# SwiGLU on one core: ScalarE's load of the first gate slices in two parts, behind its first Silu

## The chip, the core and the metric

The kernel runs on one core of a Trainium2 chip. The core has five engines with instruction queues of their own: TensorE (PE in the profile; its weight loads are listed apart as PEld), VectorE (DVE), ScalarE (ACT), GpSimd (POOL) and SyncE (SP). SP, ACT and POOL also issue DMAs from their queues. The metric is device time in microseconds, lower is better.

## The reference

```python
B, S, D, F = 1, 2048, 640, 1536      # all bf16
def reference(x, w_gate, w_up, w_down):
    g = _silu(x @ w_gate)            # [S, D] @ [D, F]
    u = x @ w_up
    return (g * u) @ w_down          # [S, F] @ [F, D]
```

## The kernel before

The rows of x are worked in four blocks of 512 (`S_BLK`, NSB = 4). D = 640 is cut into KD = 5 pieces of 128 (the contraction index `kd`, 0 to 4), F = 1536 into KF = 12 slices of 128 (the index `fc`). All weights stay in SBUF: `wg_sb` and `wu_sb` as [128, 5, 1536], `wd_sb` as [128, 12, 640]. x is held turned over, as `xT` [128, 5, 2048].

For each block and slice TensorE makes the gate product `pg` and the up product `pu` (5 matmuls each, `proj`, L205), ScalarE takes Silu of `pg` into `sg` (L222), and VectorE multiplies `sg` by `pu` into `aT` (L223). When the 12 slices of a block are done, TensorE makes the last 128 output columns turned over (`po_t`, L285) and then, for four groups of 128 rows, the first 512 columns (`po_a`, L314); ScalarE casts them and they are stored. Beside this VectorE works out the last four rows' products by itself (L154), in time that it has free.

The head is written out by hand, and each engine keeps the order in which its instructions are written (`keep_order`):

- The first 256 rows of x come as two chunks: chunk 0 by SP and chunk 1 by ACT, 160 KB each (L88). TensorE runs 20 small matmuls on a constant (`warm`, L183) and then turns the two chunks over (L196, ten transposes through `pt`). Of each chunk ScalarE copies the pieces 0 and 1 into `xT`, VectorE the pieces 2 to 4 (L201).
- Rows 256 to 511 come turned over by two transposing DMAs on SP (`turn_x`, L112), for pieces 0 to 2 and 3 to 4.
- Four gate slices (`N_FIRST`) come before all others. Slices 0 and 1 come in two parts: pieces 0 and 1 by SP, 128 KB, and pieces 2 to 4 by ACT, 192 KB. Slices 2 and 3 follow: pieces 0 and 1 by POOL, 128 KB, pieces 2 to 4 by SP, 192 KB (all at L118). `load_k(engine, tile, source, a, b, k0, k1)` loads slices a to b-1 of pieces k0 to k1-1.
- TensorE then runs the early matmuls of slices 0 and 1 (L247): pieces 0 and 1 on chunk 0, the same on chunk 1 (eight matmuls of 128 columns), and then piece 2 for both slices, piece 3, piece 4, on all 256 columns (six matmuls). Slices 2 and 3 follow on the same 256 columns (ten matmuls at L205), then the four slices on rows 256 to 511 (20 matmuls, those of pieces 0 to 2 first), and then the up products of the four slices.
- ScalarE's queue in the head: the DMA of chunk 1, the DMA of pieces 2 to 4 of gate slices 0 and 1, a Silu of a [128, 1] constant (`silu_first`, L128) whose result nobody reads and in front of which the table load stands, then the two copies of L201, and from there the Silus of L222.

The constants that matter are `K_CUT = 2`, `X_CUT = 3`, `PE_X = 2` and `N_FIRST = 4`.

Of the kernel before, what the change touches and what calls it, by code (L numbers as in the profile page):

```python
# [10 lines left out]
def _body(  # L11
# [8 lines left out]
    nc = tc.nc  # L20
# [3 lines left out]
    ACT = mybir.ActivationFunctionType  # L24
# [8 lines left out]
    KD = D // P  # L33
# [10 lines left out]
    K_CUT = 2  # L44
    X_CUT = 3
# [15 lines left out]
    wg_sb = consts.tile([P, KD, F], bf16)  # L61
# [15 lines left out]
    wg_v = w_gate.rearrange("(kd p) f -> p kd f", p=P)  # L77
# [3 lines left out]
    def wslice(a, b):  # L81
        return slice(a * P, b * P)
# [23 lines left out]
    ones = consts.tile([P, 1], bf16)  # L106
    silu_first = consts.tile([P, 1], f32)
# [8 lines left out]
    def load_k(eng, dst, src, a, b, k0, k1):  # L116
        f_sl = wslice(a, b)
        eng.dma_start(out=dst[:, k0:k1, f_sl], in_=src[:, k0:k1, f_sl])  # L118

    load_k(nc.sync, wg_sb, wg_v, 0, 2, 0, K_CUT)  # L120
    load_k(nc.scalar, wg_sb, wg_v, 0, 2, K_CUT, KD)
    load_k(nc.gpsimd, wg_sb, wg_v, 2, N_FIRST, 0, K_CUT)
    load_k(nc.sync, wg_sb, wg_v, 2, N_FIRST, K_CUT, KD)
    turn_x(PE_X, SUB, 0, X_CUT)
    turn_x(PE_X, SUB, X_CUT, KD)
    load_k(nc.sync, wu_sb, wu_v, 0, N_FIRST, 0, X_CUT)
    load_k(nc.sync, wu_sb, wu_v, 0, N_FIRST, X_CUT, KD)
    nc.scalar.activation(silu_first[:], ones[:, 0:1], ACT.Silu)  # L128
    for a, b in W_CHUNKS:
        load_w(nc.sync, wg_sb, wg_v, a, b)  # L130
        load_w(nc.sync, wu_sb, wu_v, a, b)
# [277 lines left out]
def kernel(tc, *args):  # L409
    _body(tc, *args)  # L410
    tc.close()
    tc.compile()
    _trim(tc.nc)
# [30 lines left out]
```

## Time and profile before

| | |
|---|---|
| Median of 3 runs | 163.34 us (163.30 to 163.34) |
| The profiled execution | 163.38 us, of which the profile's span is 162.0 us |
| TensorE busy | 159.1 us, 98% of the span |
| VectorE, ScalarE, GpSimd busy | 110.8, 42.6, 1.5 us |
| DMA | 15.86 MB; 36.9% of the 16 engines' span on SP's queue (q1), 3.4% on ACT's (q10) |

Of the page, part 2 shows the span in 40 slices, part 4 the chain of work that ended last, part 5 the groups of instructions and part 6 the DMA issues with the time from issue to landing. "Idle before" is the time for which an engine stood still in front of an instruction, and the name behind the arrow is what ended it. A line that begins with SPq, ACTq or a POOL DMA is the time in which the queue issued the DMA, not the time in which the bytes moved.

### The profile page before, as it was taken

The page shows a single profiled execution, that of the slowest core. Times are in us where ns is not written, and L with a number is a line of the kernel's source. Part 1 is how long each engine was busy: PE and PEld are TensorE (multiplying, and loading weights), DVE is VectorE, ACT ScalarE, POOL GpSimd, SP SyncE. Part 2 cuts the span into 40 slices and gives each one's busy share as a digit, 9 for nine tenths or more (in the row PEclk, how much of TensorE's full clock was granted, in tenths as well). Part 3 has the DMA queues.
Part 4 walks back from the last instruction along what each step waited for, and adds up shares of the span by engine and source line. Part 5 has one row for each costly group of instructions (what it writes and reads, how often), then busy time and mean ns, then how long its engine had stood idle before and what let it go on. Part 6 is the DMA issues. An engine that isn't in the chain of part 4 may idle for free.

```text
span 162.0 us, 2107 instructions
## 1 busy us (share of the span) xinstructions
PE 159.1 (98%) x786; PEld 78.0 (48%) x798; DVE 110.8 (68%) x249; ACT 42.6 (26%) x74; POOL 1.5 (1%) x7
## 2 busy tenths in 40 slices
PE   9999999999999999999999999999999999999995
PEld 8854444444444444444444444444444444445454
DVE  1034223599469999979919999979964999993000
ACT  5051222112222222221222322221214222222121
POOL 3000000000000000000000000000000000000000
PEclk9999999999999999999999999999999999999999
DMA  7999999993179993002110000000320000000212
GB/s 226 266 360 354 362 213 230 228 208 83 35 185 161 216 212 69 4 0 34 65 65 0 0 4 2 0 0 3 62 68 33 0 0 0 0 0 4 51 38 73
DMA packets 41609, 15.86 MB, mean 98 GB/s; under 512 B 33248, under 2 KB 41440, under 8 KB 41600
## 3 DMA queue, kind: packets, MB, share of 16 engines
q1 hardware_dynamic: 33072, 14.75, 36.9%
q10 hardware_dynamic: 8480, 0.85, 3.4%
q8 instruction: 6, 0.10, 0.3%
q0 software_dynamic: 48, 0.13, 0.2%
q14 instruction: 3, 0.02, 0.1%
HBM read 6.88 MB, written 2.62 MB: 59 GB/s over the span
## 4 chain that ended last, share of the span: by engine, by line
PE 98%; issue 1%; DVE 0%
PE pu L205 32%; PE pg L205 31%; PE po_a L314 26%; PE po_t L285 6%; PE pw L183 1%; PE pg L247 1%; PE pt L196 1%; DVE ot_b L326 0%; DVE ones L108 0%
## 5 line engine op out<-in xcount | busy, mean ns | idle before, releaser
L205 PE MATMUL pu<-xT,wu_sb 128*128 128x512 bf16 (+1 forms) x239 | 59.0, 379 | 0.1
L205 PE MATMUL pg<-xT,wg_sb 128*128 128x512 bf16 (+2 forms) x244 | 57.7, 365 | 0.3
L223 DVE TENSOR_TENSOR aT<-sg,pu 128x512 bf16<-128x512 f32 (+1 forms) x48 | 32.8, 683 | 32.5 <-PE pu L205 32.5
L222 ACT ACTIVATE sg<-pg 128x512 f32<-128x512 f32 (+1 forms) x48 | 28.4, 596 | 71.2 <-PE pg L205 67.1
L314 PE MATMUL po_a<-wd_sb,aT 128*128 128x512 bf16 (+2 forms) x212 | 42.4, 358 | 0.2
L154 DVE SCALAR_TENSOR_TENSOR prod<-wgT,x_row 128x640 f32<-128x640 bf16 x48 | 39.4, 821 | 1.1
L154 DVE SCALAR_TENSOR_TENSOR prod<-wuT,x_row 128x640 f32<-128x640 bf16 x48 | 39.4, 822 | 1.0
L205 PEld LDWEIGHTS <-wg_sb 128*128 128x128 bf16 x250 | 24.5, 98 | 26.2
L205 PEld LDWEIGHTS <-wu_sb 128*128 128x128 bf16 x240 | 23.5, 98 | 28.0
L314 PEld LDWEIGHTS <-aT 128*128 128x128 bf16 x216 | 20.7, 98 | 21.6
L323 ACT CAST ot<-po_a 128x512 bf16<-128x512 f32 (+1 forms) x17 | 9.5, 560 | 32.0 <-PE po_a L314 20.9
L285 PE MATMUL po_t<-aT,wd_sb 128*128 128x512 bf16 (+1 forms) x47 | 10.3, 365 | 0.1
L285 PEld LDWEIGHTS <-wd_sb 128*128 128x128 bf16 x48 | 4.7, 98 | 5.1
L326 DVE CAST ot_b<-po_a 128x128 bf16<-128x128 f32 x1 | 0.3, 291 | 9.9 <-PE po_a L314 9.9
L294 ACT CAST ot_t<-po_t 128x512 bf16<-128x512 f32 (+1 forms) x4 | 2.2, 558 | 11.6 <-PE po_t L285 11.6
L154 DVE DVE_READ_ACCUMULATOR prod<-wuT,x_row 128x1 f32 x48 | 3.9, 82 | 0.0
L154 DVE DVE_READ_ACCUMULATOR prod<-wgT,x_row 128x1 f32 x48 | 3.9, 82 | 0.0
L296 DVE STREAM_TRANSPOSE ot_q<-ot_t 128x512 bf16<-128x512 bf16 (+1 forms) x4 | 2.7, 679 | 1.7 <-ACT ot_t L294 1.7
L201 DVE COPY xT<-pt 128x384 bf16<-128x384 bf16 x2 | 0.7, 359 | 3.2 <-PE pt L196 3.2
L183 PE MATMUL pw<-ones 128*128 128x128 bf16 x20 | 2.3, 313 | 0.3 <-DVE ones L108 0.3
L247 PE MATMUL pg<-xT,wg_sb 128*128 128x128 bf16 (+1 forms) x14 | 2.3, 340 | 0.0
L183 PEld LDWEIGHTS <-ones 128*128 128x128 bf16 x20 | 2.1, 147 | 0.3 <-DVE ones L108 0.3
(16 smaller groups left out, 8.3 us busy)
## 6 DMA issues: line engine op xcount, KB each, us to landing
wd_sb<-in_w_down_dram SPq DMA_DIRECT2D x1, 1920.0 KB, 14.2
out_dram<-ot SPq DMA_DIRECT2D x15, 128.0 KB, 1.7
wg_sb<-in_w_gate_dram SPq DMA_DIRECT2D x2, 640.0 KB, 7.3
wu_sb<-in_w_up_dram SPq DMA_DIRECT2D x2, 640.0 KB, 8.7
x_row<-in_x_dram SPq DMA_DIRECT2D x1, 640.0 KB, 4.9
wu_sb<-in_w_up_dram SPq DMA_DIRECT2D x1, 384.0 KB, 3.8
out_dram<-ot_q ACTq DMA_DIRECT2D x12, 32.0 KB, 1.9
wu_sb<-in_w_up_dram SPq DMA_DIRECT2D x1, 256.0 KB, 4.0
```

The lines of the kernel that those rows point to most:

```text
L154: nc.vector.scalar_tensor_tensor(out=prod[:], in0=wT[:, fc, :], scalar=1.0, in1=x_row[:, t, :], op0=ALU.mult, op1=ALU.mult, accum_out=acc[ ...
L183: nc.tensor.matmul(pw[:, 0:P], lhsT=ones[:].broadcast_to([P, P]), rhs=ones[:].broadcast_to([P, P]), start=True, stop=True,)
L196: nc.tensor.transpose(out=pt[:, kd - k0, :], in_=x_sb[:, c, kd * P : (kd + 1) * P], identity=ident[:],)
L205: nc.tensor.matmul(ps[:, c0:c1], lhsT=w_sb[:, kd, fc * P : (fc + 1) * P], rhs=xT[:, kd, sb * S_BLK + c0 : sb * S_BLK + c1], start=(kd == 0 ...
L222: nc.scalar.activation(sg[:, 0:n_s], pg[:, 0:n_s], ACT.Silu)
L223: nc.vector.tensor_tensor(out=aT[:, fc, s0 : s0 + n_s], in0=sg[:, 0:n_s], in1=pu[:, 0:n_s], op=ALU.mult)
L247: nc.tensor.matmul(pgs[fc][:, c0:c1], lhsT=wg_sb[:, kd, wslice(fc, fc + 1)], rhs=xT[:, kd, c0:c1], start=(kd == 0 and c0 == 0), stop=(kd = ...
L285: nc.tensor.matmul(po_t[:], lhsT=wd_sb[:, kf, DA:D], rhs=aT[:, kf, sb * S_BLK : sb * S_BLK + n_t], start=(kf == 0), stop=(kf == KF - 1),)
L294: nc.scalar.copy(ot_t[:], po_t[:])
L296: nc.vector.transpose(out=ot_q[:], in_=ot_t[:])
L314: nc.tensor.matmul(po[:], lhsT=aT[:, kf, s0 : s0 + P], rhs=wd_sb[:, kf, c0:c1], start=(kf == 0), stop=(kf == KF - 1),)
L323: nc.scalar.copy(ot[:], po[:])
```

## The change

ScalarE's Silu of the constant moves from behind all the loads of the head to the place right behind ScalarE's first DMA (chunk 1 of x). The DMA of pieces 2 to 4 of gate slices 0 and 1 stands behind it and becomes two: piece 2, 64 KB, and pieces 3 and 4, 128 KB. The other queues are not touched, and what is computed is the same.

```diff
     load_k(nc.sync, wg_sb, wg_v, 0, 2, 0, K_CUT)
-    load_k(nc.scalar, wg_sb, wg_v, 0, 2, K_CUT, KD)
+    nc.scalar.activation(silu_first[:], ones[:, 0:1], ACT.Silu)
+    load_k(nc.scalar, wg_sb, wg_v, 0, 2, K_CUT, X_CUT)
+    load_k(nc.scalar, wg_sb, wg_v, 0, 2, X_CUT, KD)
     load_k(nc.gpsimd, wg_sb, wg_v, 2, N_FIRST, 0, K_CUT)
     load_k(nc.sync, wg_sb, wg_v, 2, N_FIRST, K_CUT, KD)
     turn_x(PE_X, SUB, 0, X_CUT)
     turn_x(PE_X, SUB, X_CUT, KD)
     load_k(nc.sync, wu_sb, wu_v, 0, N_FIRST, 0, X_CUT)
     load_k(nc.sync, wu_sb, wu_v, 0, N_FIRST, X_CUT, KD)
-    nc.scalar.activation(silu_first[:], ones[:, 0:1], ACT.Silu)
```

## The prediction

> **What bounds the kernel.** I read the chain of work that ended last first, the whole span and then its beginning in order of time (start, length, what):
>
> ```profile
> PE 98%; issue 1%; DVE 0%
> ...
> 0.30 2.32 PE pw L183 x20
> 2.62 1.13 PE pt L196 x10
> 3.75 2.08 PE pg L247 x14
> 5.82 3.27 PE pg L205 x30
> ```
>
> TensorE is the chain: from 0.30 us on it hardly stops, and behind the head nothing that it waits for is longer than 0.05 us. Nothing downstream has room to take up a delay, so a microsecond that TensorE loses in the first 6 us is a microsecond at the end, and the question is only what the change does to those 6 us.
>
> Next the timeline of the head (start, length, engine, line, operation; idle time before it in brackets):
>
> ```profile
> 0.13 0.40 ACTq L88 DMA_DIRECT2D x_sb<-in_x_dram  x1
> 0.56 0.45 ACTq L118 DMA_DIRECT2D wg_sb<-in_w_gate_dram  x1
> 1.04 1.28 ACT L128 ACT_TABLE_LOAD   x1 [1.04 <-issue]
> 2.33 0.20 ACT L128 ACTIVATE silu_first<-ones 128x1 f32<-128x1 bf16 x1
> 2.93 0.37 ACT L201 COPY xT<-pt 128x256 bf16<-128x256 bf16 x1 [0.40 <-PE pt L196]
> ...
> 4.56 0.98 PEld L247 LDWEIGHTS <-wg_sb 128*128 128x128 bf16 x6 [0.23 <-DMA wg_sb<-in_w_gate_dram]
> 5.55 3.27 PEld L205 LDWEIGHTS <-wg_sb 128*128 128x128 bf16 x30
> ```
>
> TensorE's weight loads stand 0.23 us before 4.56, for a DMA of the gate weights. Which one, the DMA view tells (queue, size, us from issue to landing):
>
> ```profile
> wg_sb<-in_w_gate_dram ACTq DMA_DIRECT2D x1, 192.0 KB, 4.0
> wg_sb<-in_w_gate_dram SPq DMA_DIRECT2D x1, 192.0 KB, 4.2
> x_sb<-in_x_dram ACTq DMA_DIRECT2D x1, 160.0 KB, 2.7
> wg_sb<-in_w_gate_dram SPq DMA_DIRECT2D x1, 128.0 KB, 2.9
> wg_sb<-in_w_gate_dram POOLq DMA_DIRECT2D x1, 128.0 KB, 4.3
> ```
>
> ACT's 192 KB: issued at 0.56, landed 0.56 + 4.0 = 4.56, the moment the weight load begins. The load that the change touches is the one transfer that TensorE already waits for; it has no slack at all, and 0.23 us is the most that an earlier landing could give.
>
> **The change, part by part.** All on ScalarE's queue.
>
> *The Silu in front.* The table load takes the place of the DMA issue, at 0.56: 0.56 + 1.28 = 1.84, and the Silu runs to about 1.85 + 0.20 = 2.05. No price of its own: it ended at 2.53 before, 0.40 before the first copy (2.93), and nobody reads its result.
>
> *The two loads behind it.* Does a DMA issue wait until the instructions in front of it on its engine are done? No row shows it on ScalarE. Bounds: it goes out at about 0.6 if it doesn't wait, at about 2.08 if it does. The nearest row is GpSimd's:
>
> ```profile
> 0.65 0.29 POOL masks.py:199 TENSOR_SCALAR_AFFINE_SELECT ident<-ident 128x128 bf16<-128x128 bf16 x1
> ...
> 1.01 0.83 POOL L118 DMA_DIRECT2D wg_sb<-in_w_gate_dram  x1
> ```
>
> The select ended at 0.94, and the DMA, which needs nothing of it, started 0.07 later. On ScalarE the opposite order is seen to be strict too (DMA issue to 1.01, table load from 1.04). By these rows I take "it waits": piece 2 is issued from 2.08 to about 2.48 (an issue takes 0.40 to 0.45 here), pieces 3 and 4 from 2.51 to about 2.94. The price of one more DMA is that second issue, 0.43 us of ScalarE's queue; the copy queued behind moves from 2.93 to 2.97, and the first L247 matmul, which reads it at 3.54 (the copy ends 3.30), doesn't feel it.
>
> The Trainium skill (Advanced Engine Details and Errata, Sequencer Loop) says otherwise: an engine instruction is pushed into a queue, waits there, and the sequencer reads on. By it the loads would go out at about 0.6, which is the first rival below.
>
> *Landing.* Rows for an issue in this head: 2.5 us (chunk 0, nothing in front), 2.7 (chunk 1), 2.9 (SP's 128 KB), and for those issued from 0.9 on 4.2, 4.3, and for the two transposes 4.4 (issued 1.43) and 3.5 (issued 2.77). Piece 2 finds ACT's queue empty: 2.7 by chunk 1, the smallest row of this queue, so 2.08 + 2.7 = 4.78; ends 4.6 and 6.3. Pieces 3 and 4, issued at 2.51, lie between 2.7 and 4.2: 5.2 to 6.7. The nearest in time is the transpose issued at 2.77 (3.5), the nearest in kind SP's 128 KB (2.9); I take 3.3, so 5.8.
>
> *What TensorE does with that.* It is ready for piece 2 at 4.56 - 0.23 = 4.33. Before, six matmuls of 256 columns ran from 4.57 to 5.66, when the first L205 matmul starts. Their starts (4.57, 4.97, 5.18, 5.39, then 5.55, 5.66) show 0.21 us each up to about 5.5 and 0.11 after; the 30 of L205 take 3.27 / 30 = 0.109. TensorE's rate doubles at about 5.5 us, though the granted clock is shown as 1.00 throughout. With the change: piece 2 at 4.78, two matmuls to 5.21, a stop until 5.8, then four matmuls at the fast rate, 4 x 0.109 = 0.44, to 6.24. Against 5.66 that is +0.58 us. Ends: landing at 5.2 gives 5.80 (one and a half matmuls at the slow rate, the rest fast), +0.14; landing at 6.7 gives 7.14, +1.48.
>
> *What the moved bytes collide with.* 192 KB leave the stretch before 3.5 us and join SP's transposes and GpSimd's 128 KB. At the 0.29 MB/us of that stretch they can push the others by at most 0.66 us. The transposes land at 5.83 and 6.27 and are first read at about 6.75 and 8.06; the up weights land at 7.9 and 8.66, read at 8.94 and 9.6. Pushed by all of 0.66 the four would land at 6.49, 6.93, 8.56 and 9.32, in time even if TensorE were not late itself. Gate slices 2 and 3 (5.1 and 5.31, read at 5.55) lose a competitor. Price nothing; the least cover is that of the first transpose and of the second up load, some 0.3 us, and a push beyond it would cost what is over.
>
> Sum: +0.58 - nothing gained elsewhere. The profiled execution took 163.38 (span 162.0, 1.4 around it), so 163.96 for it; the median is 0.04 lower, so 163.92.
>
> **The rivals.**
>
> *The issue runs ahead of the Silu (not slower).* ScalarE hands the table load and the Silu on and issues piece 2 at about 0.6, pieces 3 and 4 at about 1.05. For it: nothing in the code makes these DMAs wait, and the copies in the tail of a block show only the other order. Against it: the GpSimd row. Piece 2 then lands well before 4.33 (0.6 + 2.9 = 3.5), and TensorE starts it there, 0.23 earlier. Pieces 3 and 4 now stand behind SP's 192 KB (issued 0.90, landed 5.1) and land between 1.05 + 3.5 = 4.55 and 5.1, wanted at 4.75. At 4.75 or before, the six end 0.12 earlier, since what is saved of the slow stretch is half lost where the rate would have doubled anyway; at 5.1 they end at 5.72, 0.06 later. 163.22 to 163.40, say 163.28. It decides as soon as ACT's next issue starts before 1.0 us.
>
> *The rate doubles later.* The doubling came 5.2 us after TensorE's first matmul (0.30 to 5.5), with two short stops in it. If a stop of 0.6 us starts the count anew, another 5.2 us at half rate from 5.8 cost 2.6: 163.92 + 2.6 = 166.5; if the doubling slips only by the stop, under 0.3. For it: the stop falls right in front of the doubling. Against it: 0.23 and 0.1 us of stops didn't prevent it. The Trainium skill (TensorE: Matmul & The Clock Gate, What's actually happening) has the clock released after a busy window of some 3.4 us; one more such window at half rate would be an estimated 1.7 us, 165.6. Which share of busy time the window needs isn't said there for a stop like this one.
>
> *Held back, but the late transfers land fast.* The pieces find ACT's queue empty and land after 2.5 to 2.7 us both: the low end above, +0.14, 163.5. For it: 64 and 128 KB are small, and 32 KB stores on this queue landed after 1.9. Against it: every transfer issued after 0.9 us in this head took 3.5 or more.
>
> **How the numbers follow.** Held back with a stop as worked out 0.54 (163.92, own range 163.55 to 164.9), rate later 0.09, runs ahead 0.27, lands fast 0.10. A measurement of this kernel tells about 0.2%, 0.33 us, from no change. Slower by more: 0.51 of the first, the 0.09 and a little of the others, 0.62. Faster by more than 0.33 would need the whole 0.23 and the 0.1 us for which TensorE also stands before 2.50: 0.06, nearly all from running ahead. The rest, 0.32, is within. The range goes from 163.1 (running ahead at its best) to 164.9 (landing at 6.7), which leaves out the late rate and the outermost of the gains, some 0.15.
>
> **What would show it.** The table load at about 0.56 and ACT's two L118 issues at about 2.08 and 2.51; if they start before 1.1, the first step is wrong and with it the forecast. The L247 weight loads with an idle time of about 0.45 before piece 2 and about 0.6 before piece 3, both ended by a DMA of the gate weights; the first L205 weight load at about 6.1 in place of 5.55. L205's first matmuls at 0.109 apart show that the rate rose in time; at 0.21 it is the second rival. The distance from then on to the end unchanged shows that nothing took up the delay.

## The result and the profile after

The changed kernel takes 164.11 us at the median of 22 runs (163.38 to 167.73), the kernel before 163.38 at the median of 22 (163.08 to 165.80). The ratio is 1.0039, 95% interval 1.0026 to 1.0052: slower by 0.39%, some 0.64 us. The forecast was 163.92 and slower. The time came out near it, but not by the way that the forecast gave.

The head of the changed kernel, timeline (start, length, engine, line, operation; idle time before it and what ended it in brackets):

```profile
0.57 1.28 ACT L121 ACT_TABLE_LOAD   x1 [0.57 <-issue]
0.64 0.86 ACTq L118 DMA_DIRECT2D wg_sb<-in_w_gate_dram  x2
...
1.86 0.20 ACT L121 ACTIVATE silu_first<-ones 128x1 f32<-128x1 bf16 x1
...
2.87 0.37 ACT L202 COPY xT<-pt 128x256 bf16<-128x256 bf16 x1 [0.81 <-PE pt L197]
...
3.68 0.98 PEld L248 LDWEIGHTS <-wg_sb 128*128 128x128 bf16 x10 [0.26 <-DMA wg_sb<-in_w_gate_dram]
...
5.61 0.33 PEld L248 LDWEIGHTS <-wg_sb 128*128 128x128 bf16 x4 [0.95 <-DMA wg_sb<-in_w_gate_dram]
```

The first two lines overlap. ScalarE's table load runs from 0.57 to 1.85, and both gate loads are issued inside it, from 0.64 to 1.50 (the first takes 0.38). Here the DMA issues didn't wait for the table load and the Silu in front of them. The last line is where the loss comes from: the weight loads of pieces 3 and 4 stand for 0.95 us. The line at 3.68 has a smaller stop, 0.26 us, for SP's first gate load, which landed at 3.64 (3.41 before); so piece 2, though landed, was used at 4.51, hardly earlier than the 4.57 of before.

The DMA issues (queue, size, us from issue to landing):

```profile
wg_sb<-in_w_gate_dram SPq DMA_DIRECT2D x1, 192.0 KB, 4.8
...
wg_sb<-in_w_gate_dram POOLq DMA_DIRECT2D x1, 128.0 KB, 4.5
wg_sb<-in_w_gate_dram ACTq DMA_DIRECT2D x1, 128.0 KB, 4.5
wg_sb<-in_w_gate_dram ACTq DMA_DIRECT2D x1, 64.0 KB, 3.2
```

Piece 2 lands at 0.64 + 3.2, about 3.8, well before TensorE can use it. Pieces 3 and 4, issued when the first issue is done at about 1.05, land 4.5 later, at 5.57. Before, all three had landed at 4.52.

The chain in order of time names the same transfer:

```profile
1.05 4.52 DMA wg_sb<-in_w_gate_dram
5.57 0.05 issue
5.61 0.61 PE pg L248 x4
6.22 3.27 PE pg L206 x30
9.50 0.21 PE pu L206
```

The 30 matmuls that began at 5.82 in this view before begin at 6.22, 0.40 later, and the span is 162.4 in place of 162.0. Nothing behind takes the delay up. That these 30 take 3.27 as before says that TensorE's rate had doubled by then; the four in front of them, from 5.61 on, start 0.11 apart, where matmuls before 5.5 us started 0.21 apart. That is a part of why a stop of 0.95 costs only 0.40; the other is the wait of 0.23 that was there before.

### The profile page after: what moved, and what is told of

The parts are those of the page before. It is cut to its first block, busy times and chain, and to the rows that moved or that the text cites. A ratio compares the mean times of both kernels' runs of the same rounds, so it can differ in the third digit from the quotient of the medians.

```text
span 162.4 us, 2108 instructions
## 1 busy us (share of the span) xinstructions
PE 159.0 (98%) x786; PEld 77.7 (48%) x798; DVE 110.7 (68%) x249; ACT 42.6 (26%) x74; POOL 1.5 (1%) x7
## 3 DMA queue, kind: packets, MB, share of 16 engines
HBM read 6.88 MB, written 2.62 MB: 59 GB/s over the span
## 4 chain that ended last, share of the span: by engine, by line
PE 95%; DMA 3%; issue 1%; ACT 0%; ACTq 0%; DVE 0%
PE pu L206 32%; PE pg L206 31%; PE po_a L315 26%; PE po_t L286 6%; DMA wg_sb<-in_w_gate_dram 3%; PE pg L248 0%; ACT L121 0%; ACTq L88 0%; DVE ot_b L327 0%
## 5 line engine op out<-in xcount | busy, mean ns | idle before, releaser
L206 PE MATMUL pu<-xT,wu_sb 128*128 128x512 bf16 (+1 forms) x239 | 59.0, 379 | 0.1
L206 PE MATMUL pg<-xT,wg_sb 128*128 128x512 bf16 (+2 forms) x244 | 57.7, 366 | 0.3
L206 PEld LDWEIGHTS <-wg_sb 128*128 128x128 bf16 x250 | 24.5, 98 | 26.2
L206 PEld LDWEIGHTS <-wu_sb 128*128 128x128 bf16 x240 | 23.5, 98 | 28.0
L286 PE MATMUL po_t<-aT,wd_sb 128*128 128x512 bf16 (+1 forms) x47 | 10.3, 365 | 0.1
```

Source lines behind the costliest of these rows:

```text
L206: nc.tensor.matmul(ps[:, c0:c1], lhsT=w_sb[:, kd, fc * P : (fc + 1) * P], rhs=xT[:, kd, sb * S_BLK + c0 : sb * S_BLK + c1], start=(kd == 0 ...
L286: nc.tensor.matmul(po_t[:], lhsT=wd_sb[:, kf, DA:D], rhs=aT[:, kf, sb * S_BLK : sb * S_BLK + n_t], start=(kf == 0), stop=(kf == KF - 1),)
```

## The experiments

Two theories stood at first. S: the split is what costs, since the second load is issued 0.45 us later, behind SP's 192 KB. T: the table load beside the DMA issues is what costs. Line numbers below are those of each kernel. "Landing" is issue plus the time to landing; a transfer is counted in 16 shares, and it has landed with the last of them. The edits of the first two experiments and of the last three are shown against the kernel before, the others against the changed kernel.

**The split alone.**

```diff
-    load_k(nc.scalar, wg_sb, wg_v, 0, 2, K_CUT, KD)
+    load_k(nc.scalar, wg_sb, wg_v, 0, 2, K_CUT, X_CUT)
+    load_k(nc.scalar, wg_sb, wg_v, 0, 2, X_CUT, KD)
```

> The Silu stays in its old place, only the one load of pieces 2 to 4 becomes two (piece 2, then 3 and 4). Theory S (the split makes it slow: the second load is issued some 0.45 us later, its bytes come behind SP's 192 KB and meet the transposes): pieces 3 and 4 issued near 1.0, landed at 5.2 to 5.6, time 163.8 to 164.3, as with the whole change. Theory T (the table load that runs beside the DMA issues makes it slow): pieces 3 and 4 land by 4.6 to 4.9 and the time stays at 163.2 to 163.5. In both the table load starts near 1.4 and the first copy moves by at most 0.1 us.

164.16 us, ratio 1.0068 (1.0035 to 1.0101). Its timeline:

```profile
0.56 0.93 ACTq L118 DMA_DIRECT2D wg_sb<-in_w_gate_dram  x2
...
1.52 1.28 ACT L129 ACT_TABLE_LOAD   x1 [1.52 <-issue]
...
6.07 0.33 PEld L248 LDWEIGHTS <-wg_sb 128*128 128x128 bf16 x4 [1.47 <-DMA wg_sb<-in_w_gate_dram]
```

With the table load behind both issues the stop is there all the same, 1.47 us. The Silu isn't needed for the loss.

**The Silu in front alone.**

```diff
+    nc.scalar.activation(silu_first[:], ones[:, 0:1], ACT.Silu)
     load_k(nc.scalar, wg_sb, wg_v, 0, 2, K_CUT, KD)
...
-    nc.scalar.activation(silu_first[:], ones[:, 0:1], ACT.Silu)
```

> Only the Silu moves to the front, the 192 KB stay one load. Theory S: the load is issued near 0.64 in place of 0.56 and lands at 4.5 to 4.7, time 163.2 to 163.6, as before. Theory T: landing at 5.2 or later and 163.8 or more. The issue time also tells once more whether a DMA issue waits for the Silu in front of it (near 0.64 if not, near 2.08 if it does).

163.25 us, ratio 0.9996 (0.9982 to 1.0009): nothing that can be told from no change. Timeline, and below it the DMA issues:

```profile
0.56 1.28 ACT L121 ACT_TABLE_LOAD   x1 [0.56 <-issue]
0.63 0.40 ACTq L118 DMA_DIRECT2D wg_sb<-in_w_gate_dram  x1
```

```profile
wg_sb<-in_w_gate_dram ACTq DMA_DIRECT2D x1, 192.0 KB, 4.1
```

The load goes out 0.07 later than before and lands at 0.63 + 4.1, about 4.75. Theory T falls, and the Silu's new place costs next to nothing.

**Cut one piece later** (pieces 2 and 3, then 4).

```diff
-    load_k(nc.scalar, wg_sb, wg_v, 0, 2, K_CUT, X_CUT)
-    load_k(nc.scalar, wg_sb, wg_v, 0, 2, X_CUT, KD)
+    load_k(nc.scalar, wg_sb, wg_v, 0, 2, K_CUT, X_CUT + 1)
+    load_k(nc.scalar, wg_sb, wg_v, 0, 2, X_CUT + 1, KD)
```

> As the change, but cut one piece later: pieces 2 and 3 (128 KB), then piece 4 (64 KB). Theory S: the first part lands at 4.0 to 4.5 and the second, still behind SP's 192 KB, at 5.0 to 5.5, but TensorE wants it only at about 5.2, so the stop shrinks from 0.95 to at most 0.3 us: 163.3 to 163.7. Rival (the late shares come with any second load, whatever its size): the second part at 5.5 or later, 163.7 to 164.1.

163.72 us, ratio 1.0019 (1.0005 to 1.0033). Piece 4, only 64 KB, lands at 5.96. So the lateness isn't a matter of size, the landing went as the rival said and the time lies where both ranges meet. Over its runs it costs less than the split alone (1.0068); that only two matmuls are left to wait for piece 4 is the likely reason, which wasn't tried by itself.

**The swap.** SP loads pieces 3 and 4 of slices 0 and 1 as its third load, ScalarE the 192 KB of slices 2 and 3.

```diff
     load_k(nc.scalar, wg_sb, wg_v, 0, 2, K_CUT, X_CUT)
-    load_k(nc.scalar, wg_sb, wg_v, 0, 2, X_CUT, KD)
+    load_k(nc.sync, wg_sb, wg_v, 0, 2, X_CUT, KD)
+    load_k(nc.scalar, wg_sb, wg_v, 2, N_FIRST, K_CUT, KD)
     load_k(nc.gpsimd, wg_sb, wg_v, 2, N_FIRST, 0, K_CUT)
-    load_k(nc.sync, wg_sb, wg_v, 2, N_FIRST, K_CUT, KD)
```

> The Silu in front and piece 2 on ScalarE as in the change, but SP loads pieces 3 and 4 of slices 0 and 1 as its third load and ScalarE loads pieces 2 to 4 of slices 2 and 3 as its third: the wanted 128 KB stand ahead of the 192 KB. Theory S: pieces 3 and 4 land at 4.3 to 4.8, slices 2 and 3 at 5.1 to 5.7; the stop before piece 3 falls away or nearly so, time 163.1 to 163.6. A rival to S (a small load on its own lands late wherever it stands, since one of 16 shares is slow): pieces 3 and 4 at 5.2 or later again, 163.8 or more.

163.90 us, ratio 1.0038 (1.0008 to 1.0069): outside what S expected, though in the profile, of 163.59 us, pieces 3 and 4 landed at 4.82 and the stop was 0.37. A second profile was to tell why:

> The swap once more, for a second profile, since its times (163.9) were above what its first profile explains. If ScalarE's 192 KB of slices 2 and 3, now issued near 1.07, are late (the stop has moved to the next load), they land at 5.8 or later and TensorE stops before or inside the ten matmuls of slices 2 and 3. If pieces 3 and 4 are late, they land at 5.2 or later. If neither, only the point at which TensorE's rate doubles is left.

165.8 us (one run), and here pieces 3 and 4 landed at 0.91 + 5.11 = 6.02. The chain:

```profile
0.91 5.11 DMA wg_sb<-in_w_gate_dram
6.02 0.05 issue
6.07 1.04 PE pg L248 x4
7.11 4.39 PE pg L206 x30
```

Two things are to be seen. Issued at 0.91, a little ahead of ScalarE's load, these 128 KB can land at 4.82 or at 6.02. And the matmuls themselves are slow: 4 take 1.04 (0.61 in the changed kernel's chain), 30 take 4.39 (3.27). TensorE's rate doubled only at about 9.3 us here, 0.43 + 1.12 = 1.55 us lost beside the stop. S as it stood, "behind the 192 KB", was too simple: something else decides how late a load issued near 1 us lands.

**The changed kernel again.**

> The changed kernel once more, to see how far pieces 3 and 4 move from one execution to the next. Theory S: issued near 1.07 again, the last of the 16 shares lands at 5.2 to 6.0, most of them a good deal earlier, and TensorE stops before piece 3 for 0.5 us or more. Rival (the 5.57 of the first profile was one bad execution): landing under 5.0 and a time of 163.5 or less.

164.44 us over six runs, ratio 1.0100 (1.0060 to 1.0141); landing at 6.18, a stop of 1.60. Of the 16 shares of pieces 3 and 4, seven had landed by 5.13 and nine came between 6.03 and 6.18; in the first profile twelve by 4.70 and four between 5.35 and 5.57. A good part of the transfer is there about a microsecond before its last shares.

**What holds up the late shares?** In three more kernels the neighbours were moved. The transposes of x behind the up weights:

```diff
-    turn_x(PE_X, SUB, 0, X_CUT)
-    turn_x(PE_X, SUB, X_CUT, KD)
     load_k(nc.sync, wu_sb, wu_v, 0, N_FIRST, 0, X_CUT)
     load_k(nc.sync, wu_sb, wu_v, 0, N_FIRST, X_CUT, KD)
+    turn_x(PE_X, SUB, 0, X_CUT)
+    turn_x(PE_X, SUB, X_CUT, KD)
```

> The changed kernel with SP's two transposing loads of x moved behind the two loads of the up weights, so that no transposed bytes move before about 5 us. If the transposes hold up the late shares of pieces 3 and 4 (theory S with the transposes as the cause), they land at 4.5 to 5.0 and the stop before piece 3 shrinks below 0.4 us. If it is the bytes in front of them (theory S with the backlog as the cause), they land at 5.2 to 5.8 as before. The transposes themselves land near 8 in either case, after TensorE wants them (6.8), so the time is 164 or more and only the landing counts.

Pieces 3 and 4 land at 5.39 (15 shares by 4.87), in the range given for the bytes in front and outside that for the transposes; 165.78 us over four runs, with a stop of 1.2 for the transposes.

GpSimd's 128 KB loaded by SP:

```diff
-    load_k(nc.gpsimd, wg_sb, wg_v, 2, N_FIRST, 0, K_CUT)
     load_k(nc.sync, wg_sb, wg_v, 2, N_FIRST, K_CUT, KD)
+    load_k(nc.sync, wg_sb, wg_v, 2, N_FIRST, 0, K_CUT)
```

> The changed kernel with GpSimd's 128 KB (pieces 0 and 1 of slices 2 and 3) loaded by SP instead, behind its 192 KB. If GpSimd's load holds up the late shares of pieces 3 and 4, they land at 4.5 to 5.0 and the time falls to 163.2 to 163.6. If not, they land at 5.2 or later and the time stays at 163.8 to 164.3. The moved load is wanted at about 5.6 to 6.0 and should land by then.

Landing at 5.17, all 16 shares between 4.12 and that; 163.90 us, ratio 1.0041 (1.0023 to 1.0058). The expected 4.5 to 5.0 wasn't reached, and the time lies in the range given for "not" (163.8 to 164.3). Against the six runs of the changed kernel that were measured beside it (1.0060 to 1.0141) it is a little faster; against the 22 runs of the result (1.0026 to 1.0052) nothing is gained. In its profile the stop before pieces 3 and 4 is 0.44 us, and the matmuls start 0.21 apart until 6.25 in place of 5.39, so a part of what is left of the loss there isn't the landing's.

The transposes ahead of SP's 192 KB and GpSimd's 128 KB behind that on SP, so that only transposes stand between:

```diff
-    load_k(nc.gpsimd, wg_sb, wg_v, 2, N_FIRST, 0, K_CUT)
-    load_k(nc.sync, wg_sb, wg_v, 2, N_FIRST, K_CUT, KD)
     turn_x(PE_X, SUB, 0, X_CUT)
     turn_x(PE_X, SUB, X_CUT, KD)
+    load_k(nc.sync, wg_sb, wg_v, 2, N_FIRST, K_CUT, KD)
+    load_k(nc.sync, wg_sb, wg_v, 2, N_FIRST, 0, K_CUT)
```

> The changed kernel with SP's transposing loads ahead of SP's 192 KB, and GpSimd's 128 KB behind those on SP, so that nothing but the transposes stands between SP's first gate load and ScalarE's pieces 3 and 4. Backlog as the cause: pieces 3 and 4 land at 4.2 to 4.8. Transposes as the cause: at 5.2 or later. Slices 2 and 3 come too late here (near 7 or 8), so the time is 165 or more and only the landing of pieces 3 and 4 counts.

Landing at 4.72, all shares between 4.27 and that, in the range given for the bytes in front; GpSimd's load is away too, so this kernel doesn't tell the two apart. 164.93 us (one run), as slices 2 and 3 come too late.

The same is seen in the queues. The DMA view of 4.6 to 6.2 us (packets that start there, MB, share of the 16 engines; each packet counts with its whole time, so a share can exceed 100%; q1 is SP's queue, q10 ScalarE's, q0 GpSimd's) for the changed kernel, first the second profile of it, then that without GpSimd's load:

```profile
q1 hardware_dynamic: 779, 0.22, 106.6%
q10 hardware_dynamic: 91, 0.04, 9.0%
q0 software_dynamic: 20, 0.05, 7.1%
```

```profile
q1 hardware_dynamic: 1152, 0.30, 124.2%
```

With GpSimd's load, 91 packets of ScalarE's gate load and 20 of GpSimd's start in that stretch (13 and 3 in the first profile of the change); without it, none do.

Each of the three moves brought the landing forward, from 5.57 and 6.18 to 5.39, 5.17 and 4.72. But that is one profile each, and the two profiles of the changed kernel lie 0.61 apart, so they don't settle which neighbour has the most to do with it. Nor is it ScalarE's load alone that is held up: in the two profiles of the change the last shares of SP's 192 KB (5.74 and 6.31), of GpSimd's 128 KB (5.53 and 6.21) and of pieces 3 and 4 (5.57 and 6.18) come close together.

**The load whole, but late.** This separates the split from the place: chunk 1 of x is cut instead, so that the 192 KB go out as one load at 1.11.

```diff
-    load_x(nc.scalar, 1, 2)
+    for d0, d1 in ((0, K_CUT * P), (K_CUT * P, D)):
+        nc.scalar.dma_start(out=x_sb[:, 1:2, d0:d1], in_=x_v[:, 1:2, d0:d1])
...
+    nc.scalar.activation(silu_first[:], ones[:, 0:1], ACT.Silu)
     load_k(nc.scalar, wg_sb, wg_v, 0, 2, K_CUT, KD)
...
-    nc.scalar.activation(silu_first[:], ones[:, 0:1], ACT.Silu)
```

> The 192 KB of pieces 2 to 4 stay one load, with the Silu in front of it, but ScalarE's load of chunk 1 of x is cut into two (64 and 96 KB), so that the gate load is issued about 0.43 us later, near 1.05, with no byte more in front of it. If what costs is the later place in the order of issue (behind SP's 192 KB, issued at 0.90), the load lands at 5.2 to 6.0, TensorE stops before piece 2 for about 1 us, and the time is 163.8 to 164.6. If what costs is that the load is in two parts, it lands at 4.5 to 4.9 and the time is 163.2 to 163.6.

166.93 us, ratio 1.0232 (1.0198 to 1.0266), worse than either range. Its chain:

```profile
1.11 5.77 DMA wg_sb<-in_w_gate_dram
6.88 0.05 issue
6.93 1.46 PE pg L248 x6
8.39 4.27 PE pg L206 x30
```

One load of 192 KB issued 0.55 later than before lands at 6.88, 2.4 later. It is the place in the order of issue, not the cut. And behind the stop of 2.8 us TensorE is back at its slow rate: 30 matmuls in 4.27, with a granted clock of 0.50 from 7 to 10 us.

**GpSimd's load away from the kernel before.** By SP behind its 192 KB:

```diff
-    load_k(nc.gpsimd, wg_sb, wg_v, 2, N_FIRST, 0, K_CUT)
     load_k(nc.sync, wg_sb, wg_v, 2, N_FIRST, K_CUT, KD)
+    load_k(nc.sync, wg_sb, wg_v, 2, N_FIRST, 0, K_CUT)
```

> The kernel before with GpSimd's 128 KB loaded by SP behind its 192 KB; ScalarE's load whole and early. If GpSimd's load is what holds up the late shares in the kernel before too, ScalarE's load lands at 4.3 to 4.6 with a shorter tail and slices 2 and 3 by 5.3, time 162.9 to 163.3. If it is not, the time stays within 0.3 of that of before; the transposes are issued 0.45 later and land at about 6.0 and 6.5, before they are wanted.

Or by ScalarE as its third, with the Silu in front:

```diff
+    nc.scalar.activation(silu_first[:], ones[:, 0:1], ACT.Silu)
     load_k(nc.scalar, wg_sb, wg_v, 0, 2, K_CUT, KD)
-    load_k(nc.gpsimd, wg_sb, wg_v, 2, N_FIRST, 0, K_CUT)
+    load_k(nc.scalar, wg_sb, wg_v, 2, N_FIRST, 0, K_CUT)
...
-    nc.scalar.activation(silu_first[:], ones[:, 0:1], ACT.Silu)
```

> The kernel before with the Silu in front and GpSimd's 128 KB loaded by ScalarE as its third load, behind the whole 192 KB. ScalarE's gate load lands at 4.5 to 4.7 as before, the moved 128 KB, issued near 1.07, at 5.2 to 5.8 like every load issued there, wanted at about 5.6: 163.1 to 163.6. If the loads issued near 1.07 are late because of GpSimd's load (now gone), it lands by 5.0 and the time is 162.9 to 163.3.

163.51 us, ratio 1.0007 (0.9992 to 1.0023), and 163.34 us, ratio 1.0004 (0.9992 to 1.0016): no difference, both. ScalarE's gate load lands at 4.11 and 4.42, earlier than the 4.52 of before, and in the second kernel the 128 KB issued near 1.05 land at 5.24 with all shares between 5.08 and that. That misses the landing by 5.0 which was expected if GpSimd's load is the cause of the late landing; what is gone is the spread of the shares. No kernel beat the one before.

The landing of the load that went out on ScalarE at 1.03 to 1.11, over the profiles:

| kernel | load | last share | GpSimd's load |
|---|---|---|---|
| the change, two profiles | 128 KB | 5.57, 6.18 | there |
| split alone | 128 KB | 6.03 | there |
| cut one later | 64 KB | 5.96 | there |
| swap, two profiles | 192 KB | 5.77, 6.58 | there |
| whole but late | 192 KB | 6.88 | there |
| transposes behind | 128 KB | 5.39 | there |
| GpSimd's by SP | 128 KB | 5.17 | by SP |
| only transposes between | 128 KB | 4.72 | by SP, later |
| before, ScalarE's third | 128 KB | 5.24 | none, it is this one |

In the eight profiles with GpSimd's load the last share comes 1.3 to 2.5 us behind the first one; in the three without, 0.2 to 1.05. That goes with GpSimd's load, but doesn't show it as the cause: with it three loads go out between 0.9 and 1.11 us, without it two, and three loads there of which none is GpSimd's weren't tried. One profile speaks for GpSimd's: in that of the Silu alone two go out there, SP's 192 KB and GpSimd's, and five of the 16 shares of SP's 192 KB land at 5.14 to 5.61, the others by 4.49. The kernel before has the same two, and there SP's 192 KB has landed by 5.12.

## Why the prediction came out right, point by point

*What bounds the kernel*: right for this change. ScalarE's gate load was the transfer TensorE waited for, and the 0.40 us that it cost in the head was found again in the span. That each microsecond lost in the head is one at the end isn't so: a stop of 0.90 us in the profile of the Silu alone cost nothing (below).

*"It waits"*: wrong, and this is the step that failed. By GpSimd's row I put the two issues at 2.08 and 2.51; they started at 0.64 and 1.05, inside the table load. The runs showed in its place that ScalarE hands the table load and the Silu on and goes to the DMA (at 0.61 to 0.64 in every profile in which the Silu stands in front of its second DMA). The Trainium skill (Advanced Engine Details and Errata, Sequencer Loop) had it so: an engine instruction is pushed into a queue and the sequencer reads on; the trace agrees with 0.07 us between the table load's start and the issue. GpSimd's row didn't carry over; why its DMA waited wasn't tried.

*Landing*: piece 2 was forecast at 4.78 and landed at 3.81, so the stop before it never came. Pieces 3 and 4 were forecast at 5.8 and landed at 5.57 and 6.18. Two errors met: issued 1.46 us earlier than I thought, they took 4.5 and 5.1 us in place of 3.3. That the two nearly cancel, and with them the time comes out near the forecast, is luck. I had taken 2.7 to 4.2 as the bounds of a landing. All eight profiles with GpSimd's load beside this one exceed 4.2 (4.4 to 5.8); the three without lie between 3.7 and 4.2.

*What TensorE does*: +0.58 forecast. Of the six matmuls two ran early and four at the fast rate, as worked out, and the first L206 matmul came at 6.06 in place of 5.66, +0.40, with +0.64 over all runs.

*What the moved bytes collide with*: priced at nothing for the others, and none of the others that were named became a wait. But gate slices 2 and 3, said to lose a competitor, landed later (5.74 and 5.53 in place of 5.12 and 5.28), still ahead of their use at 5.95; and the collision fell on the load itself, which I hadn't priced.

*The Silu in front costs nothing*: right, 0.9996.

*Rival "the issue runs ahead"*: its mechanism is what happened, its price isn't. It put the landing of pieces 3 and 4 at 4.55 to 5.1 by taking SP's 192 KB, 5.1, as the latest. The order held in both profiles of the change, but SP's 192 KB itself came at 5.74 and 6.31, and pieces 3 and 4 were 0.5 to 1.1 later than 5.1. Nor did TensorE start piece 2 0.23 earlier (4.51 in place of 4.57). So 164.11 was measured in place of 163.28.

*Rival "the rate doubles later"*: not in the profiles of the change, but in two of the experiments. In the swap's second profile it cost 1.55 us against 2.6 by my row. The Trainium skill (TensorE: Matmul & The Clock Gate, What's actually happening) names a busy window of some 3.4 us that runs freely, from which the estimate was 1.7; the kernel with the load whole but late agrees, with the granted clock up from about 3.46 us, down to 0.50 from 6.88 and up again at 10.3, 3.4 us each. Whether the highest times of the change (up to 167.73) are such executions wasn't seen, as no profile fell on one.

*Rival "the late transfers land fast"*: didn't happen with GpSimd's load in place; the kernel with only transposes between, 4.72, is the nearest to it.

What stays open: what holds up the late shares, GpSimd's load or a third load near 1 us, and how. No profile here shows the shares by engine.

## What to carry to other kernels

Where a load is already waited for, cutting it in two puts the second part one issue (0.4 us here) later in the order, and what else is in flight then can put its landing off: ask which transfers' bytes it will now share the engines with, and count on the last of its 16 shares, not on the mean. A DMA behind an activation on ScalarE that needs nothing of it wasn't held by it here. And a gain that is limited to a 0.23 us wait is small beside what a place lost in a full DMA stretch can cost.

## What the runs showed that was not expected

- The point at which TensorE's rate doubles moves from one execution to the next, at equal code: 6.0 us in one profile of the swap and 9.3 in the other; 4.3 us or earlier, 5.5 and 6.3 in profiles of kernels that take the same time to 0.2% (the Silu alone; before; before with GpSimd's load by SP). In the Silu-alone profile TensorE stood 0.90 us for SP's first gate load, and the span was still 161.9, since the rate was double from 4.33 on. Single profiles of this kernel can't be compared below some 0.5 us without knowing this point.
- The granted clock doesn't show the slow rate at the start (it is 1.00 in the kernel before from 4.6 to 5.4 us, with matmuls 0.21 apart), but does in the middle. Of the kernel with the load whole but late, the clock row of the 40 slices (4.14 us each):

```profile
PEclk9879999999999999999999999999999999999999
```

Of the pages that have this row it is the only one with anything but nines, and its second and third slice, 4.14 to 12.4 us, hold the slow stretch from 6.88 to 10.3 behind TensorE's stop.
